# Loads of the mixed up-projection weights issued from ACT's queue instead of SP's

## The chip, the cores and the metric

The kernel runs on one core of a Trainium2 chip. The metric is the device time of one execution in microseconds; the kernel before takes 936.96 us in the median of three runs (936.65 to 940.6). The engines are named as in the profile: PE (matrix products), PEld (PE's weight loads), DVE, ACT, POOL, and SP, which computes nothing and issues DMAs. An engine's name with a q (SPq, ACTq) is its sequencer, which waits for semaphores and issues DMAs.

## The reference

Attention with random features, and a feed-forward pair of products behind it:

```python
q_s, k_s = (q * scale, k * scale)
def phi(x):
    proj = np.einsum('bhsd,md->bhsm', x, omega)
    sq = np.sum(x * x, axis=-1, keepdims=True) / 2.0
    h = proj - sq
    h = h - np.max(h, axis=-1, keepdims=True)
    return np.exp(h) / np.sqrt(m)
q_p, k_p = (phi(q_s), phi(k_s))
kv = np.einsum('bhsm,bhsd->bhmd', k_p, v)
z = np.sum(k_p, axis=2)
num = np.einsum('bhsm,bhmd->bhsd', q_p, kv)
den = np.einsum('bhsm,bhm->bhs', q_p, z)[..., None] + 1e-06
x = (num / den).transpose(0, 2, 1, 3).reshape(B * S, H * D)
h = x @ w_in
return np.maximum(0.01 * h, h) @ w_out
```

There are 8 batches of 576 tokens, 8 heads of 64, 128 features; x is 4608 by 512, w_in 512 by 2048, w_out 2048 by 512. Everything is float32 outside; inside, each float32 number is held as two float16 parts, and a product is three float16 products.

## The kernel before, in words

The 4608 tokens go in nine blocks of 512 (`NB`). For each block the kernel makes attention features of keys and queries (`Unit`, `key_batch`, `query_block`), turns the result so that the model dimension lies on the partitions, multiplies by w_in (up), applies the leaky ReLU and multiplies by w_out (down). Blocks 0 to 2 use plain products (line 1268). From block 3 (`FIRST_S`) on the up-projection uses seven products of half-size blocks in place of eight (`seven_products`, line 1178 the matrix products); from block 8 the down-projection does so too (line 1102, otherwise line 1292).

The seven products need sums and differences of blocks of w_in. `mixed_weights` makes them once and writes them, split into float16 parts, to a scratch in DRAM, `w1s` (line 979 and a line before it). `seven_products` reads them back in every block from 3 on: for each of four column groups `phi` it loads four tiles of kind "wt", two of 128 by 1024 and two of 128 by 768 words of four bytes (line 1161, in `loaded`). One group is held over to the next block, so there are 76 such loads. They go into tiles whose last readers are products of an earlier group, so a load waits for PE; the first nine also wait for the scratch.

In a group `phi` of `seven_products` three PSUM banks take turns. Product 1 goes into bank "c", and ACT or DVE copies it out (`keep`, line 375 in `high`); product 2 goes into "a"; product 6 goes into "c" again, and so on. The copy out of "c" and the next use of "c" are thus one product apart, which is 12 matrix products. What is copied out is added to other products by DVE (line 1193), passes the leaky ReLU on ACT (line 1201, or 375 and 1201), and is split into two float16 parts, the second one on POOL or DVE (line 381).

DMAs that turn a tile (DMA_TRANSPOSE) are on the way of attention: line 604 turns the scaled keys or queries into `att_t`, of which there is one tile, that PE reads in line 618; line 864 turns query features (`att_qp`); line 830 turns the attention result (`fix_xt`). All of them, the loads of keys, queries and values (lines 573, 716), the writes of the result (lines 1301, 1128) and the 76 loads of line 1161 are issued by SP.

The order of everything is computed at build time by `Plan.order`: each operation has a cost on each engine, and the plan takes the operation that can start first; `op("SP", 0.45, ...)` books 0.45 us on SP. The engines' instruction streams are then written out in that order, each engine running its own stream strictly in order and waiting on semaphores for the others. Completion of DMAs is told by eight semaphores used in turn, so that a DMA also waits for the one eight places before it in the order written out.

Of the kernel before, what the change touches and what calls it, by code (L numbers as in the profile page):

```python
# [95 lines left out]
class Plan:  # L96
# [17 lines left out]
    def buf(self, kind):  # L114
        b = Buf(kind)
        self.kinds.setdefault(kind, []).append(b)
        return b
# [166 lines left out]
def act(n, pointers=0):  # L284
    return 0.19 + n / 1190 + 0.09 * pointers


def dve(n):
    return 0.15 + n / 930
# [15 lines left out]
def performer_ffn(ctx: ExitStack, tc, qT, kT, qn, kn, vn, omT, eye, w_in, w_out, out):  # L305
    nc = tc.nc
# [54 lines left out]
    def op(engine, cost, run, port=False, **of):  # L361
        return ways([(engine, cost, run, port or engine == "POOL")], **of)

    def high(n, dst, src, scale=None, psum=False, **of):

        pointer = scale is not None and not isinstance(scale, float)
        value = (lambda: scale()) if pointer else (lambda: scale)

        def dve_run():
            if scale is None:  # L370
                nc.vector.tensor_copy(dst(), src())
            else:
                nc.vector.tensor_scalar(dst(), src(), value(), None, op0=ALU.mult)
        return ways([
            ("ACT", act(n, int(pointer)), lambda: nc.scalar.activation(dst(), src(), AF.Copy,  # L375
             scale=1.0 if scale is None else value()), False),
            ("DVE", dve(n) if psum else dve2(n), dve_run, not psum)], **of)

    def low_(n, dst, a, b, engines=("DVE",), **of):

        return ways([(e, c, lambda g=g: g.tensor_tensor(dst(), a(), b(), op=ALU.subtract), True)  # L381
                     for e, c, g in (("POOL", pool_(n), nc.gpsimd), ("DVE", stt(n), nc.vector)) if e in engines], **of)

    def at(b):
        return tiles[b.kind][b.place]
# [68 lines left out]
    class Weight:  # L454
# [92 lines left out]
        def keys(self, i):  # L547
            return [(self.parts[i], 0), (self.parts[i], 1)]
# [389 lines left out]
    def unit(tile_, u):  # L938

        return tile_.bitcast(F16).rearrange("p (u i f) -> p u i f", u=4, i=2)[:, u]  # L940
# [206 lines left out]
    def seven_products(j, gs, part, top, work, finish=None):  # L1147

        turn = turn_of(j)
        banks_, rows_, sets = {}, {}, {}
        if turn[0] in held_w1s:
            sets[turn[0]] = held_w1s.pop(turn[0])

        def loaded(phi):
            if phi not in sets:
                sets[phi] = [buf("wt") for _ in range(4)]
                for q in range(4):
                    n = 1024 if q % 2 == 0 else 768  # L1160
                    op("SP", 0.45, lambda q=q, n=n: nc.sync.dma_start(out=at(sets[phi][q])[:, :n],
                       in_=w1s[4 * phi + q, :, :n]), r=[("w1s", phi, q // 2, x) for x in UNIT if UNIT[x][0] == q % 2],
                       w=[sets[phi][q]], prio=0.0, moved=P * n * 4)
            return sets[phi]

        def product(phi, n, bank, first=False, last=False):
            q, u = UNIT[n]
            wb = [loaded(phi)[2 * c + q] for c in range(2)]
            if (phi, bank) not in banks_:
                banks_[phi, bank] = buf("ffn")  # L1170
            b = banks_[phi, bank]

            def run():
                for a in range(2):
                    o, i = at(b)[:, 256 * a:256 * a + 256], 0
                    for c in range(2):
                        for wp, xp in ((0, 0), (0, 1), (1, 0)):
                            nc.tensor.matmul(o, unit(at(wb[c]), u)[:, wp, P * a:P * a + P], mixes[j, c][n][1](xp),  # L1178
                                             start=(first and a == 0 and i == 0), stop=(a == 1 and i == 5),
                                             skip_group_check=True)  # L1180
                            i += 1
            plan.like("ffn", 1.5)
            op("PE", 12 * 0.1095, run, r=[*wb, mixes[j, 0][n][0], mixes[j, 1][n][0]], w=[b], prio=work)
            plan.like()
            return b

        def keep(b):
            g = buf("row")
            high(512, lambda: at(g), lambda: at(b), psum=True, r=[b], w=[g], prio=top - 1.0)
            return g  # L1190

        def added(g, b):
            op("DVE", dve(512), lambda: nc.vector.tensor_tensor(at(g), at(g), at(b), op=ALU.add), r=[b], w=[g], prio=top - 1.0)  # L1193

        def done(g, src, phi, side, h):

            f = 8 * side + 2 * phi
            out = lambda i: at(gs[f // 4]).bitcast(F16).rearrange("p (f i t) -> p f i t", f=4, i=2)[
                :, f % 4:f % 4 + 2, i, 256 * h:256 * h + 256]
            wide = lambda: at(g).rearrange("p (f t) -> p f t", f=2)  # L1200
            op("ACT", act(512), lambda: nc.scalar.activation(at(g), at(src), AF.Prelu, scale=H_DOWN_D if finish else H_DOWN_S,  # L1201
               alpha=0.01),
               r=[src], w=[g], prio=top - (0.0 if src is g else 0.5))
            if finish:
                finish(g, phi, side, h)
                return
            keys = lambda i: [(gs[f // 4], x, i, h) for x in (f, f + 1)]
            high(512, lambda: out(0), wide, r=[g], w=keys(0), prio=top)
            low_(512, lambda: out(1), wide, lambda: out(0), r=[g, *keys(0)], engines=("POOL", "DVE"), w=keys(1), prio=top)

        ones_ = {turn[0]: keep(product(turn[0], 1, "c", True))}
        for phi, next_ in zip(turn, (*turn[1:], None)):
            s1 = ones_[phi]
            b = product(phi, 2, "a", True, True)
            added(s1, b)
            done(s1, s1, phi, 0, 0)
            u2 = keep(product(phi, 6, "c"))
            d = product(phi, 7, "d", True)
            w = keep(product(phi, 5, "c"))
            added(w, d)  # L1220
            done(w, w, phi, 1, 1)
            if next_ is not None:
                ones_[next_] = keep(product(next_, 1, "c", True))
            c12, b = buf("row"), product(phi, 3, "c", last=True)
            done(c12, b, phi, 0, 1)
            b = product(phi, 4, "d", last=True)
            added(u2, b)
            done(u2, u2, phi, 1, 0)
        held_w1s[turn[3]] = sets[turn[3]]
# [9 lines left out]
    def turn_of(j):  # L1239

        return (0, 1, 2, 3) if (j - FIRST_S) % 2 == 0 else (3, 2, 1, 0)
# [162 lines left out]
```

## Time and profile before

| | |
|---|---|
| median of 3 runs | 936.96 us (936.65 to 940.6) |
| the profiled execution's own time | 939.2 us |
| its span, first to last instruction | 937.4 us |
| PE busy | 917.6 us, 98% |
| DVE, ACT, POOL busy | 709.3, 581.2, 416.6 us (76%, 62%, 44%) |
| granted TensorE clock | 0.998 |
| DMA moved | 145.92 MB, mean 156 GB/s |

The busy times say which engine has least room. The chain of waits follows the last instruction back through what released it. The list of waits says for how long an engine stood idle and what ended it. The timeline shows instructions in order of time, merged where equal ones follow each other; the bracket behind a row is the idle time before it and what ended it. For SP a row lasts from its first issue to the end of its last one, and a DMA's landing is not in it.

### The profile page before, as it was taken

Reading aid. Unit: us, or ns where it says so; the run is one execution under the profiler, and the core shown is the slowest. Engines: PE = TensorE matmul, PEld = TensorE weight load, DVE = VectorE, ACT = ScalarE, POOL = GpSimd, SP = SyncE. Lnnn points to the kernel's source line nnn. Section 1 sums busy time; section 2 is a strip of 40 time slices with the busy share of each in tenths; the row PEclk is TensorE's granted clock in tenths of the full one; section 3 lists DMA queues with packets and bytes.
Section 4 is the critical chain, followed back from the end, with each engine's and each line's share of the span. In section 5 each row is a group of like instructions: output and inputs, shape, how many; then the busy total and the mean of one; then the engine's idle time right before and its main releaser. Section 6 shows DMA issues by size and latency. Waiting matters only on the chain.

```text
span 937.4 us, 21163 instructions
## 1 busy us (share of the span) xinstructions
PE 917.6 (98%) x8608; PEld 612.7 (65%) x8608; DVE 709.3 (76%) x1275; ACT 581.2 (62%) x866; POOL 416.6 (44%) x380
## 2 busy tenths in 40 slices
PE   8899999999999999999999999999998999999998
PEld 6789455555555445578557855785577647845887
DVE  7789987878996877989888897876878421285773
ACT  4778777657764876568656864687567514622650
POOL 2332633557657664226332554247024722574541
PEclk9999999999999999999999999999999999999999
DMA  9754547583576789789777977496849832721301
GB/s 362 254 182 142 173 113 175 101 200 88 116 170 144 163 170 225 180 182 230 158 140 161 246 176 141 130 238 152 163 115 226 174 79 94 195 57 31 133 1 45
DMA packets 257729, 145.92 MB, mean 156 GB/s; under 512 B 191328, under 2 KB 237152, under 8 KB 256608
## 3 DMA queue, kind: packets, MB, share of 16 engines
q1 hardware_dynamic: 257632, 144.58, 63.8%
q8 instruction: 67, 1.10, 0.5%
q14 instruction: 30, 0.25, 0.1%
HBM read 81.36 MB, written 16.78 MB: 105 GB/s over the span
## 4 chain that ended last, share of the span: by engine, by line
PE 86%; DVE 6%; DMA 5%; issue 1%; ACT 1%; SPq 0%; POOL 0%; DVEq 0%; ACTq 0%
PE fixps_ffn L1292 31%; PE fixps_ffn L1178 19%; PE fixps_ffn L1268 11%; PE attps_pj L618 5%; PE lateps_ffn L1292 3%; PE lateps_ffn L1178 3%; PE lateps_ffn L1102 2%; DMA fix_big<-w_in 2%; PE fixps_ffn L1102 2%; PE attps_mi L785 2%; DVE fix_wt L495 2%; PE attps_pj L682 1%; PE attps_mi L895 1%; DMA att_t<-att_z 1%; DMA fix_xt<-fix_xn 1%
## 5 line engine op out<-in xcount | busy, mean ns | idle before, releaser
L1292 PE MATMUL fixps_ffn<-fix_wt,fix_big 128*128 128x512 f16 x1392 | 313.1, 379 | 0.0
L381 POOL TENSOR_TENSOR fix_big<-fix_row,fix_big 128x512 f16<-128x512 f32 x132 | 164.8, 1257 | 215.1 <-ACT fix_big L375 202.1
L1292 PEld LDWEIGHTS <-fix_big 128*128 128x128 f16 x1536 | 145.6, 98 | 166.2
L1178 PEld LDWEIGHTS <-fix_wt 128*128 128x128 f16 x2016 | 194.7, 98 | 26.4 <-issue 1.3
L1178 PE MATMUL fixps_ffn<-fix_xt,fix_wt 128*128 128x256 f16 x1800 | 204.5, 273 | 0.9 <-DVE fix_row L1193 0.9
L1268 PE MATMUL fixps_ffn<-fix_xt,fix_wt 128*128 128x512 f16 x576 | 129.5, 379 | 0.1
L637 ACT ACTIVATE att_p<-att_p,shift 128x1024 f32<-128x1024 f32 (+1 forms) x68 | 69.6, 1029 | 44.7 <-DVE att_p L634 44.7
L1268 PEld LDWEIGHTS <-fix_wt 128*128 128x128 f16 x576 | 54.6, 98 | 62.4
L381 DVE TENSOR_TENSOR att_ph<-att_p,att_ph 128x1024 f16<-128x1024 f32 x56 | 76.7, 1370 | 16.0 <-ACT att_ph L375 14.4
L375 ACT ACTIVATE fix_big<-fix_row 128x512 f16<-128x512 f32 x138 | 83.6, 621 | 7.5 <-DVE att_sc L584 3.6
L381 POOL TENSOR_TENSOR fix_xn<-fix_x,fix_xn 128x512 f16<-128x512 f32 (+1 forms) x36 | 43.6, 1210 | 98.8 <-ACT fix_xn L375 96.2
L625 DVE TENSOR_REDUCE att_st<-attps_pj 128x8 f32<-128x1024 f32 x68 | 73.0, 1074 | 15.1 <-PE attps_pj L618 14.9
L1193 DVE TENSOR_TENSOR fix_row<-fix_row,fixps_ffn 128x512 f32<-128x512 f32 x64 | 43.8, 684 | 50.0 <-PE fixps_ffn L1178 26.4
L634 DVE SCALAR_TENSOR_TENSOR att_p<-attps_pj,att_sc,att_st 128x1024 f32<-128x1024 f32 x68 | 76.7, 1132 | 0.4
L375 ACT ACTIVATE att_ph<-att_p 128x1024 f16<-128x1024 f32 x56 | 58.6, 1047 | 2.1 <-PE attps_mi L799 1.2
L576 ACT ACTIVATE att_z<-att_nat 128x512 f32<-128x512 f32 (+1 forms) x56 | 36.2, 646 | 33.9 <-DMA att_t<-att_z 26.8
L1201 ACT ACTIVATE fix_row<-fix_row 128x512 f32<-128x512 f32 x70 | 43.6, 624 | 17.5 <-DVE fix_row L1193 17.2
L618 PE MATMUL attps_pj<-om,att_t 64*128 64x128 f16 x1416 | 50.1, 217 | 4.4 <-DMA att_t<-att_z 4.4
L578 DVE TENSOR_REDUCE att_sq<-att_z 128x8 f32<-128x512 f32 (+1 forms) x56 | 39.4, 707 | 19.0 <-ACT att_z L576 18.7
L618 PEld LDWEIGHTS <-att_t 64*128 64x128 f16 x1416 | 39.7, 94 | 20.6 <-issue 13.3
L375 ACT ACTIVATE fix_row<-fixps_ffn 128x512 f32<-128x512 f32 x62 | 36.7, 592 | 24.7 <-PE fixps_ffn L1178 21.2
L375 ACT ACTIVATE fix_row<-fixps_ffn,fix_s 128x512 f32<-128x512 f32 x28 | 19.1, 684 | 50.0 <-PE fixps_ffn L1292 50.0
(187 smaller groups left out, 1645.8 us busy)
## 6 DMA issues: line engine op xcount, KB each, us to landing
fix_wt<-w1s SPq DMA_DIRECT2D x38, 512.0 KB, 4.7
fix_wt<-w1s SPq DMA_DIRECT2D x38, 384.0 KB, 3.6
att_v<-vn SPq DMA_DIRECT2D x16, 650.0 KB, 5.4
out<-fix_row SPq DMA_DIRECT2D x35, 256.0 KB, 2.3
fix_big<-w_in SPq DMA_DIRECT2D x8, 1024.0 KB, 11.3
fix_big<-w_out SPq DMA_DIRECT2D x8, 1024.0 KB, 5.2
att_nat<-qn SPq DMA_DIRECT2D x32, 256.0 KB, 3.2
w1s<-fix_y SPq DMA_DIRECT2D x32, 128.0 KB, 2.4
```

What stands on the lines that cost most here:

```text
L375: ("ACT", act(n, int(pointer)), lambda: nc.scalar.activation(dst(), src(), AF.Copy, scale=1.0 if scale is None else value()), False),
L381: return ways([(e, c, lambda g=g: g.tensor_tensor(dst(), a(), b(), op=ALU.subtract), True) for e, c, g in (("POOL", pool_(n), nc.gpsimd), ...
L578: op("DVE", dve(n), lambda: nc.vector.tensor_reduce(at(self.sq).rearrange("p (h c) -> p c h", h=2)[:, :nt], square().rearrange("p (c h d) ...
L618: nc.tensor.matmul(at(pj)[:, 512 * h + c * M:512 * h + (c + 1) * M], at(self.t)[r, 2 * (c0 + c) + x, :], om[r, w, :], start=(x + w == 0), ...
L625: op("DVE", dve(n * M), lambda: nc.vector.tensor_reduce(row(0), pv(), axis=AX.X, op=ALU.max), r=[pj], w=[st], prio=prio)
L634: op("DVE", dve(n * M), lambda: nc.vector.scalar_tensor_tensor(p(), pv(), down(), row(2).rearrange("p (g o) -> p g o", o=1).broadcast_to([ ...
L637: op("ACT", act(n * M, 1), lambda: nc.scalar.activation(flat(p()), flat(p()), AF.Exp, bias=shift), w=[p32], r=["ones"], prio=prio)
L1178: nc.tensor.matmul(o, unit(at(wb[c]), u)[:, wp, P * a:P * a + P], mixes[j, c][n][1](xp), start=(first and a == 0 and i == 0), stop=(a == 1 ...
L1193: op("DVE", dve(512), lambda: nc.vector.tensor_tensor(at(g), at(g), at(b), op=ALU.add), r=[b], w=[g], prio=top - 1.0)
L1201: op("ACT", act(512), lambda: nc.scalar.activation(at(g), at(src), AF.Prelu, scale=H_DOWN_D if finish else H_DOWN_S, alpha=0.01), r=[src], ...
L1268: nc.tensor.matmul(at(ph), wk[wp][:, c:c + P], xt[:, xp, :], start=(i == 0), stop=(i == 3 * KT - 1))
L1292: nc.tensor.matmul(at(po), part(f, gp)[:, t * P:(t + 1) * P], wf[wp], start=(n == 0 and f % 4 == 0 and gp == wp), stop=(n == 3 and f % 4 = ...
```

## The change

In `loaded`, the call that issues the load names the scalar engine (ACT) in place of the sync engine (SP). The planner's entry is left: the operation is still planned as 0.45 us on SP, so the order written out of all operations is the same, and only the stream into which the 76 DMA instructions go differs.

```diff
                 for q in range(4):
                     n = 1024 if q % 2 == 0 else 768
-                    op("SP", 0.45, lambda q=q, n=n: nc.sync.dma_start(out=at(sets[phi][q])[:, :n],
+                    op("SP", 0.45, lambda q=q, n=n: nc.scalar.dma_start(out=at(sets[phi][q])[:, :n],
                        in_=w1s[4 * phi + q, :, :n]), r=[("w1s", phi, q // 2, x) for x in UNIT if UNIT[x][0] == q % 2],
```

The streams of PE, DVE and POOL hold the same instructions in the same order as before. SP's stream, in the stretch between 731 and 815 us of the trace, before; `fix_xt` are turned attention results, `fix_wt` the tiles of the mixed weights:

```order
L1301 DMA out<-fix_row_2_94 128x512
L1301 DMA out<-fix_row_4_96 128x512
L1161 DMA fix_wt_1_65<-w1s_123 128x768
L1161 DMA fix_wt_7_71<-w1s_123 128x1024
L1161 DMA fix_wt_3_67<-w1s_123 128x768
L1161 DMA fix_wt_16_80<-w1s_123 128x1024
L1161 DMA fix_wt_5_69<-w1s_123 128x768
L1161 DMA fix_wt_11_75<-w1s_123 128x1024
L1161 DMA fix_wt_9_73<-w1s_123 128x768
L1161 DMA fix_wt_12_76<-w1s_123 128x1024
L1161 DMA fix_wt_1_65<-w1s_123 128x768
L1161 DMA fix_wt_3_67<-w1s_123 128x1024
```

and SP's stream from the same place after the change:

```order
L1301 DMA out<-fix_row_2_94 128x512
L1301 DMA out<-fix_row_4_96 128x512
L830 DMA_TRANSPOSE fix_xt_0_98<-fix_xn_0_86 128x4x128
L830 DMA_TRANSPOSE fix_xt_1_99<-fix_xn_1_87 128x8x128
L830 DMA_TRANSPOSE fix_xt_3_101<-fix_xn_0_86 128x8x128
```

The loads are gone from SP's stream, and the turning of `fix_xt` follows the writes of the result at once.

ACT's stream, at the first four of these loads (about 786 us), before; `fixps_ffn` are PSUM banks:

```order
L375 ACTIVATE fix_row_0_92<-fixps_ffn_1_112 128x512
L375 ACTIVATE fix_row_3_95<-fixps_ffn_0_111 128x512
L1201 ACTIVATE fix_row_0_92<-fix_row_0_92 128x512
L1201 ACTIVATE fix_row_2_94<-fixps_ffn_1_112 128x512
L375 ACTIVATE fix_big_1_89<-fix_row_0_92 128x2x256
L375 ACTIVATE fix_big_0_88<-fix_row_2_94 128x2x256
L1201 ACTIVATE fix_row_5_97<-fix_row_5_97 128x512
```

and after:

```order
L375 ACTIVATE fix_row_0_92<-fixps_ffn_1_112 128x512
L1161 DMA fix_wt_1_65<-w1s_123 128x768
L1161 DMA fix_wt_7_71<-w1s_123 128x1024
L375 ACTIVATE fix_row_3_95<-fixps_ffn_0_111 128x512
L1201 ACTIVATE fix_row_0_92<-fix_row_0_92 128x512
L1201 ACTIVATE fix_row_2_94<-fixps_ffn_1_112 128x512
L375 ACTIVATE fix_big_1_89<-fix_row_0_92 128x2x256
L375 ACTIVATE fix_big_0_88<-fix_row_2_94 128x2x256
L1161 DMA fix_wt_3_67<-w1s_123 128x768
L1161 DMA fix_wt_16_80<-w1s_123 128x1024
L1201 ACTIVATE fix_row_5_97<-fix_row_5_97 128x512
```

The first pair now stands directly ahead of a copy out of a PSUM bank, the second ahead of a leaky ReLU. At 703 us of the trace a pair that stood on SP ahead of two turnings of `att_qp` and `att_t` goes into ACT's stream in the same way:

```order
L375 ACTIVATE att_ph_167<-att_p_1_165 128x1024
L1161 DMA fix_wt_73<-w1s 128x768
L1161 DMA fix_wt_80<-w1s 128x1024
L1201 ACTIVATE fix_row_95<-fix_row_95 128x512
L1201 ACTIVATE fix_row_93<-fix_row_93 128x512
```

Here the pair follows the copy of the query features (`att_ph`), and a leaky ReLU comes behind it.

## Rows read from the trace of the kernel before

**Rows 1.** The page's busy times (part 1: busy us, share of the span, instructions) and its chain by engine (part 4).

```profile
PE 917.6 (98%) x8608; PEld 612.7 (65%) x8608; DVE 709.3 (76%) x1275; ACT 581.2 (62%) x866; POOL 416.6 (44%) x380
...
PE 86%; DVE 6%; DMA 5%; issue 1%; ACT 1%; SPq 0%; POOL 0%; DVEq 0%; ACTq 0%
```

**Rows 2.** The list of waits, of PE alone: who waited for whom, us in total, times, longest.

```profile
PE attps_pj L618 <- DMA att_t<-att_z: 4.4, 3, 2.8
...
PE fixps_ffn L1178 <- DVE fix_row L1193: 0.9, 1, 0.9
```

**Rows 3.** The timeline of PE at its three longest stops behind 328 us: start, us, what; in brackets the idle time before.

```profile
500.43 0.78 PE L618 MATMUL attps_pj<-om,att_t 64*128 64x128 f16 x21 [0.84 <-DMA att_t<-att_z]
...
549.33 0.92 PE L1178 MATMUL fixps_ffn<-fix_xt,fix_wt 128*128 128x256 f16 x7 [0.85 <-DVE fix_row L1193]
...
712.79 0.84 PE L618 MATMUL attps_pj<-om,att_t 64*128 64x128 f16 x24 [2.79 <-DMA att_t<-att_z]
```

**Rows 4.** The chain of waits in order of time at two of these stops: start, us, what.

```profile
536.33 4.41 DMA fix_xt<-fix_xn
...
542.10 2.37 DVE att_v L381
...
703.45 0.78 PE attps_pj L618 x24
704.23 2.43 PE fixps_ffn L1178 x22
706.65 6.10 DMA att_t<-att_z
```

**Rows 5.** The waits of SP's own sequencer.

```profile
SPq L1161 <- PE fixps_ffn L1178: 63.3, 23, 7.2
...
SPq L604 <- PE attps_pj L618: 31.5, 18, 3.5
```

**Rows 6.** The timeline of SP in four stretches.

```profile
492.85 1.23 SPq L864 DMA_TRANSPOSE att_qp<-att_ph  x1
494.17 1.51 SPq L830 DMA_TRANSPOSE fix_xt<-fix_xn  x1
495.79 1.26 SPq L604 DMA_TRANSPOSE att_t<-att_z  x1
...
533.90 1.03 SPq L1161 DMA_DIRECT2D fix_wt<-w1s  x2
535.03 2.75 SPq L830 DMA_TRANSPOSE fix_xt<-fix_xn  x2
...
703.60 1.00 SPq L1161 DMA_DIRECT2D fix_wt<-w1s  x2
704.70 1.84 SPq L864 DMA_TRANSPOSE att_qp<-att_ph  x1
706.65 4.01 SPq L604 DMA_TRANSPOSE att_t<-att_z  x1
...
786.26 19.15 SPq L1161 DMA_DIRECT2D fix_wt<-w1s  x10
805.96 2.71 SPq L830 DMA_TRANSPOSE fix_xt<-fix_xn  x2
```

**Rows 7.** The instructions of line 1161, and those of line 604: duration of an issue in ns (least, median, most), first and last start; and the time from issue to landing.

```profile
L1161 SPq DMA_DIRECT2D fix_wt<-w1s x76: 319/388/1765, 328.1 to 879.1; - x76
...
DMA to landing us min/median/max: 2.9/4.2/7.9
...
L604 SPq DMA_TRANSPOSE att_t<-att_z x56: 1231/1258/4523, 102.7 to 745.1; - x56
...
DMA to landing us min/median/max: 3.0/3.5/8.7
```

**Rows 8.** The timeline of ACT where pairs of loads enter its stream: at 625, 702 and 786 us.

```profile
624.64 0.71 ACT L375 ACTIVATE att_z<-att_nat,att_sc 128x512 f16<-128x512 f32 x1
625.79 0.60 ACT L375 ACTIVATE fix_row<-fixps_ffn 128x512 f32<-128x512 f32 x1 [0.43 <-PE fixps_ffn L1178]
...
701.89 1.05 ACT L375 ACTIVATE att_ph<-att_p 128x1024 f16<-128x1024 f32 x1
702.89 0.63 ACT L1201 ACTIVATE fix_row<-fix_row 128x512 f32<-128x512 f32 x1
...
786.60 0.60 ACT L375 ACTIVATE fix_row<-fixps_ffn 128x512 f32<-128x512 f32 x1 [1.50 <-PE fixps_ffn L1178]
787.91 0.60 ACT L375 ACTIVATE fix_row<-fixps_ffn 128x512 f32<-128x512 f32 x1 [0.71 <-PE fixps_ffn L1178]
```

**Rows 9.** Busy time (and count) by stretch, of the stretches in which the loads are issued: span, its length, PE, PEld, DVE, ACT, POOL, granted clock, DMA share, GB/s.

```profile
405.00:447.00 42.00, 42.00 (x528) 36.87 (x527) 36.44 (x70) 34.95 (x59) 21.29 (x20) 1.00 0.84 208
500.00:546.00 46.00, 45.57 (x542) 38.27 (x543) 38.03 (x66) 38.63 (x61) 22.80 (x20) 1.00 0.89 213
595.00:636.00 41.00, 41.00 (x478) 35.77 (x477) 32.93 (x60) 35.13 (x57) 18.76 (x18) 1.00 0.86 208
690.00:731.00 41.00, 38.21 (x446) 33.82 (x444) 29.66 (x53) 30.31 (x51) 19.70 (x18) 1.00 0.80 200
782.00:815.00 33.00, 32.93 (x309) 29.21 (x308) 7.57 (x13) 21.93 (x39) 15.66 (x14) 1.00 0.62 183
```

**Rows 10.** The chain of waits at 863 us: one product of line 1178, 12 matrix products.

```profile
863.40 1.31 PE fixps_ffn L1178 x12
```

## The prediction

> **What bounds the kernel.** I read the page's busy times first, then the chain of waits, then the list of waits, then the timelines of PE, SP and ACT. The busy times say PE: 917.6 of 937.4 us [rows 1], and the chain agrees, 86% of it being PE's own work. So nothing that only shortens a DMA or a queue can give more than PE's stops. Behind 328 us, where the first of the loads is issued [rows 7], the list of waits and the timeline give three stops worth naming: 0.84 us at 500, 0.85 us at 549 and 2.79 us at 713 [rows 2, 3], together 4.5 us. That is 0.48% of the time, and it is the ceiling of the gain.
>
> Two of the stops lead back to SP. At 713 PE waits for the turned keys or queries `att_t`. The chain goes from the landing at 712.75 back over 6.10 us of DMA to the issue at 706.65 [rows 4]. SP's timeline shows what stood there: a pair of the loads at 703.60, a turning of `att_qp` at 704.70, and then the issue of `att_t` at 706.65, which itself took 4.01 us [rows 6] against a median of 1.258 [rows 7]. The landing took 6.10 us against a median of 3.5. At 549 the chain goes through DVE back to a turning of `fix_xt` issued at 536.33 [rows 4], the second of two that stand right behind a pair of loads at 533.90 [rows 6]. The stop at 500 follows a turning issued at 495.79 that stands behind other turnings and no load of line 1161 [rows 6]. I give it no gain.
>
> **What goes from SP.** 76 issues of 0.388 us in the median (29 us of SP), and with them 63.3 us in which SP stood at one of them waiting for PE [rows 5], while later turnings stood behind it. The plainest place is 786 to 805 us, where ten loads hold SP for 19.15 us and two turnings of `fix_xt` come out at 805.96 [rows 6].
>
> At 713: without the pair, `att_qp` can be issued about 1.0 us earlier, and `att_t` behind it. `att_t` has one tile, which PE reads from 703.45 on [rows 4]; so the turning can't start before about 703.5, and with an issue of `att_qp` of 1.2 us ahead of it starts at about 704.2. That is 2.4 us before the 706.65 of now. If the landing still takes 6.10 us, the stop shrinks from 2.79 to about 0.35; if the landing falls towards 3.5 us, since the 0.9 MB of loads (128 by 1792 words of four bytes) are no longer ahead of it in the same queue, the stop goes. Gain 2.4 to 2.79; I take 2.6. Its other end is nothing, should the transfers share the same DMA time anyway.
>
> At 549: the turning comes 1.03 us earlier, the time of the pair, and the 0.85 us stop goes if everything on DVE between them (the chain has 2.37 us of `att_v` there) moves too. Gain 0 to 0.85; I take 0.5.
>
> **What comes onto ACT.** 76 issues. The trace shows none on ACT. The nearest row is SP's own: 0.319 at least, 0.388 in the median, 1.765 at most [rows 7]. A pair back to back took 0.80 to 1.03 us on SP [rows 6]. Lower bound nothing (issued while an ACTIVATE is still running), upper bound 1.765 each; I take the median, and 0.82 us a pair, since it is the same instruction.
>
> What hides it. In the stretches where the loads are issued ACT is busy 34.95 of 42, 38.63 of 46, 35.13 of 41, 30.31 of 41 and 21.93 of 33 us [rows 9], so 6 to 11 us idle, while six pairs want 4.9 us. And the pairs stand where ACT waits for PE: at 786 the pair comes behind a copy that ends at 787.20 and ahead of one that starts at 787.91 after 0.71 us of idling; at 625 the room is 0.43 us [rows 8]. If the issue may begin while the copy runs, another 0.5 us is room. A pair of 0.82 us then fits in 0.9 to 1.2; if it may not, it is late by 0.1 to 0.4 us. A late copy out of bank "c" costs PE only what goes over the room left: one product of 1.31 us [rows 10] lies between, of which the copy takes 0.60. So some 0.7 us less two hand-overs, about 0.4 us, is left. Queued behind the DMA on ACT are the copies, leaky ReLUs and high parts that DVE, POOL and PE take next. I put the whole toll at 0 to 1.5 us and take 0.6.
>
> The added wait. On ACT a load stands still until PE has read the old weights. At 786 its place is reached at about 786.7, when SP had already been able to issue it (786.26) [rows 6, 8]. At 702 ACT comes to the pair by 702.9, and SP issued it at 703.60; whether PE had let go of the tiles by then no row says, so up to 0.7 us of waiting is possible there. The plan orders ACT by the same times by which it ordered the loads, so I take no waiting. The weights land 4.2 us after issue in the median and PE has not one stop on `fix_wt<-w1s` in its list of waits; an issue some tenths later should stay hidden.
>
> **The sum.** 2.6 + 0.5 - 0.6 = 2.5 us less. Against the profiled execution's own 939.2 us (span 937.4 and 1.8 around it) that is 936.7. The median of the runs is 936.96, 2.2 us under that execution; if its stops are the same, the sum gives 934.5, and if the profiled execution was long because of its stop at 713, the gain is mostly not there to have and the time stays near 936.7. I take the middle, 935.6 us.
>
> **Rivals.**
>
> A, the forecast: turnings come earlier, one or two stops go, ACT pays little. 933 to 936.5 us. Chance 0.42.
>
> B, nothing to be measured: what is taken off SP is not what the stops wait for, because the DMA engines are shared and are 0.80 to 0.89 busy in those stretches [rows 9]; gain and toll cancel, 936.5 to 938. For it: PE's ceiling is small. Against it: the issue of 4.01 us and the place right behind a pair. The Trainium skill, in "DMA: Bandwidth & Descriptors" (Issuing engines are not separate DMA queues), says that all issuers' transfers run on the same 16 DMA engines and that issuing from several saves only the sequencer's time. By that rule the landing of 6.10 us would stay and only the 2.4 us of issue would be gained. No run here yet shows two issuers. Chance 0.28.
>
> C, the other side: issuing costs ACT far more than it cost SP, and copies out of PSUM come late. Place: the pairs directly ahead of a copy out of a bank, some 14 of the 38 by the order. Price: if each load has to wait for one turning of SP, 1.23 us [rows 7], a pair is 2.46 us; less 1.2 us of room and 0.4 us at PE it costs 0.86 us each, 12 us in all, or 949 us; at 1.765 us each it is 1.9 us each and 27 us, 964. It decides from about 0.8 us a load on. For it: the turnings ahead of the stop at 713 keep SP issuing for 1.84 and 4.01 us [rows 6], so the two issuers would often meet, and ACT is idle for only 14 to 17% of three stretches [rows 9]. Against it: SP's median of 0.388. The Trainium skill, in "Perfetto Trace Analysis" (DMA Instruction — HWDGE (DVE, Sync)), says that the block that makes the descriptors is shared, is locked by one issuer at a time, and that the wait for the lock is within the profiled interval. No trace here shows that yet; if it holds, it is what would make C true. Chance 0.22.
>
> D, contention: the loads, now beside the turnings and not ahead of them, slow each other. PE's waits for `att_t` double, 4.4 us more: 941. For it the DMA share; against it that no byte is added. Chance 0.06. That the change doesn't do what it says is excluded by the order: 76 rows left SP, 76 came to ACT. The remaining 0.02 I leave to what I don't see.
>
> **How the numbers follow.** What a measurement of this kernel can tell from no change is about 0.5%: below 932.3 us or above 941.6. Faster than that needs nearly all of the 4.5 us of stops without any toll; I give it 0.10, all from A. Slower comes from C (all but 0.02), half of D and the unseen: 0.24. The rest is 0.66. The range of 8 in 10 goes from 932, where all stops are gone, to 944, which takes in A, B, D and the mild part of C.
>
> **What would show it.** Right: PE's stop on `att_t` at 713 gone or under 0.5 us; issue of `att_t` there at about 704; line 1161 under ACTq with a median near 0.4 us; ACT's idling before copies unchanged within some tenths. Wrong: ACTq issues of 0.8 us and more, and a new line in PE's list of waits that names ACT `fix_row` L375; or PE waiting for `fix_wt<-w1s`; or the stop at 713 still there with `att_t` issued early, which would be B.

## The result and the profile after

The changed kernel takes 950.1 us in the median (948.4 to 959.8, four runs) against 936.9: a ratio of 1.0149, with a 95% interval of 1.0121 to 1.0177. It is 1.5% slower; the prediction of 935.6 us and its range up to 944 us were wrong. The profiled execution took 949.1 us (span 947.3), 9.9 us of span more than the one of before. The ratios and intervals in this document are those on record; a quotient of the medians beside them can differ by 0.002.

First the page of the changed kernel: busy times, the new queue of DMA packets (packets, MB, share of 16 engines' span) and the chain by engine, beside [rows 1].

```profile
PE 919.5 (97%) x8608; PEld 613.7 (65%) x8608; DVE 709.9 (75%) x1275; ACT 580.3 (61%) x866; POOL 418.3 (44%) x380
...
q10 hardware_dynamic: 10944, 34.87, 11.8%
...
PE 81%; DMA 8%; DVE 6%; issue 2%; ACT 2%; SPq 1%; ACTq 0%; DVEq 0%
```

The loads are a second queue, q10, with 34.9 MB. DMA in the chain went from 5% to 8%, PE from 86% to 81%, ACT from 1% to 2%.

Then PE's list of waits behind 328 us, beside [rows 2], and PE's timeline at its longest stops, beside [rows 3].

```profile
PE attps_mi L897 <- DMA att_qp<-att_ph: 5.1, 2, 3.7
PE attps_pj L618 <- DMA att_t<-att_z: 3.8, 4, 1.4
PE attps_pj L618 <- DVE att_p L634: 2.0, 1, 2.0
PE fixps_ffn L1178 <- ACT fix_row L375: 2.0, 2, 1.4
```

```profile
367.64 0.85 PE L618 MATMUL attps_pj<-om,att_t 64*128 64x128 f16 x24 [2.02 <-DVE att_p L634]
...
372.63 0.20 PE L897 MATMUL attps_mi<-fix_kv,att_qp 128*128 128x65 f16 x1 [1.39 <-DMA att_qp<-att_ph]
...
448.15 0.84 PE L618 MATMUL attps_pj<-om,att_t 64*128 64x128 f16 x24 [1.32 <-DMA att_t<-att_z]
...
455.73 0.84 PE L618 MATMUL attps_pj<-om,att_t 64*128 64x128 f16 x24 [1.42 <-DMA att_t<-att_z]
...
716.63 0.20 PE L897 MATMUL attps_mi<-fix_kv,att_qp 128*128 128x65 f16 x1 [3.67 <-DMA att_qp<-att_ph]
...
822.65 1.03 PE L1178 MATMUL fixps_ffn<-fix_xt,fix_wt 128*128 128x256 f16 x8 [1.36 <-ACT fix_row L375]
```

Summed over the trace, PE's stops behind 328 us grew from 4.56 to 12.81 us, by 8.25. The rest is clock. The windows around the longest stop show it (span, its length, PE, PEld, DVE, ACT, POOL, granted clock, DMA share, GB/s).

```profile
712.00:716.00 4.00, 0.96 (x11) 0.76 (x8) 3.93 (x4) 0.83 (x2) 2.69 (x2) 1.00 1.35 180
716.00:720.00 4.00, 3.37 (x28) 2.66 (x29) 1.23 (x5) 0.63 (x2) 0.00 (x0) 0.71 0.88 165
720.00:724.00 4.00, 4.00 (x50) 3.14 (x49) 2.62 (x9) 3.50 (x5) 0.00 (x0) 0.86 0.71 234
```

Behind the stop of 3.67 us the granted clock is 0.71 and 0.86 in two windows of 4 us. At the lower of the two levels, half speed, that is (0.29 + 0.14) x 4 / 0.5 = 3.4 us, in which 1.7 us of work are lost; PE's busy time is 1.9 us larger. The stops ahead of 328 us are 0.3 us shorter, and 8.25 + 1.9 - 0.3 make the 9.9 us. (The medians are 13.2 us apart: the profiled execution of before lies 2.3 us above its median, the one of after 1 us below its own.)

Where do the stops come from? The chain of waits of the changed kernel in order of time, in three places (start, us, what), beside [rows 4].

```profile
353.02 12.00 DMA att_t<-att_z
...
365.05 0.64 ACT att_z L576
...
438.22 1.61 ACTq L1161
...
441.67 13.41 DMA fix_xt<-fix_xn
...
708.13 8.46 DMA att_qp<-att_ph
```

Three turnings land 12.00, 13.41 and 8.46 us after their issue. Each stands beside loads on ACT's queue: five of them at 350.1 to 353.5, two at 437.9 and 438.2 and two more at 444.3 and 444.7, a pair at 708.1. Of the 129 turnings behind 328 us the median landing is 3.6 us (3.5 before), so most are untouched; but six take over 8 us, where before it was one, with 8.65 (the `att_t` that now takes 12.00).

The last place is not the stop of before grown longer. PE waited there for `att_t`; now it waits for the `att_qp` that was issued at 702.19 before, ahead of the pair on SP, and landed after 4.7 us. ACT issues the pair at the same moment as this turning (708.12 and 708.13), and it lands after 8.46 us. SP's timeline, beside [rows 6]:

```profile
705.65 6.24 SPq L864 DMA_TRANSPOSE att_qp<-att_ph  x3
712.00 4.03 SPq L604 DMA_TRANSPOSE att_t<-att_z  x1
```

`att_t` still takes 4.03 us to issue, and lands after 6.7 us (6.10 before), with no load ahead of it on SP's queue.

ACT itself, line 1161 under its own sequencer and the timeline at 708 us, beside [rows 7, 8].

```profile
L1161 ACTq DMA_DIRECT2D fix_wt<-w1s x76: 326/327/1612, 327.6 to 889.0; - x76
```

```profile
707.84 1.05 ACT L375 ACTIVATE att_ph<-att_p 128x1024 f16<-128x1024 f32 x1
708.12 0.81 ACTq L1161 DMA_DIRECT2D fix_wt<-w1s  x2
```

An issue costs 0.327 us in the median, and this pair of 0.81 us lies almost wholly under a running ACTIVATE of 1.05 us. Of the 76 issues 59 begin while an ACTIVATE runs.

So one theory is that the bytes of the loads, on a queue of their own beside SP's turnings, hold these up (overtaking or contention). The rival is that 76 issues in ACT's in-order stream make its copies late (a held ACT): two stops of after do name ACT's `fix_row`. A third is that more DMAs on shared completion counters couple the two engines.

### The profile page after: what moved, and what is told of

It reads as the page before. It is cut to its first block, busy times and chain, and to the rows that moved or that the text cites. A ratio compares the mean times of both kernels' runs of the same rounds, so it can differ in the third digit from the quotient of the medians.

```text
span 947.3 us, 21134 instructions
## 1 busy us (share of the span) xinstructions
PE 919.5 (97%) x8608; PEld 613.7 (65%) x8608; DVE 709.9 (75%) x1275; ACT 580.3 (61%) x866; POOL 418.3 (44%) x380
## 3 DMA queue, kind: packets, MB, share of 16 engines
q10 hardware_dynamic: 10944, 34.87, 11.8%
## 4 chain that ended last, share of the span: by engine, by line
PE 81%; DMA 8%; DVE 6%; issue 2%; ACT 2%; SPq 1%; ACTq 0%; DVEq 0%
PE fixps_ffn L1292 26%; PE fixps_ffn L1178 19%; PE fixps_ffn L1268 12%; PE attps_pj L618 4%; PE lateps_ffn L1292 3%; PE lateps_ffn L1178 2%; DMA att_t<-att_z 2%; PE lateps_ffn L1102 2%; DMA fix_big<-w_in 2%; DMA fix_xt<-fix_xn 2%; PE fixps_ffn L1102 2%; PE attps_mi L785 2%; PE attps_pj L682 1%; DVE fix_wt L495 1%; DMA att_qp<-att_ph 1%
## 5 line engine op out<-in xcount | busy, mean ns | idle before, releaser
L381 POOL TENSOR_TENSOR fix_big<-fix_row,fix_big 128x512 f16<-128x512 f32 x132 | 169.5, 1292 | 214.6 <-ACT fix_big L375 201.1
L381 POOL TENSOR_TENSOR fix_xn<-fix_x,fix_xn 128x512 f16<-128x512 f32 (+1 forms) x36 | 41.6, 1157 | 99.9 <-ACT fix_xn L375 98.6
```

## The experiments

**Issues on ACT without the bytes.** All loads stay on SP; at each place ACT issues a small DMA.

```
-   lambda q=q, n=n: nc.sync.dma_start(out=at(sets[phi][q])[:, :n], in_=w1s[...])
+   lambda q=q, n=n: (nc.sync.dma_start(out=at(sets[phi][q])[:, :n], in_=w1s[...]), tiny())
+   tiny = lambda: [nc.scalar.dma_start(out=bits[:, 4 * c:4 * c + 4], in_=eye[:, :4])
+                   for c in [next(spot) % 16]]
```

> All 76 loads stay on SP, as in the kernel before; at each place where a load is issued, ACT issues a DMA of its own of 128 rows of 16 bytes. The theory of overtaking (the bytes on a second queue hold up the turnings on SP's) expects the time of before within 0.3%, 935 to 940 us, and PE's stops after 328 us at 4 to 6 us. The theory of a held ACT (76 issues in ACT's stream make its copies late) expects most of the loss to be there: 945 us or more, with stops of PE on ACT fix_row. The theory of shared completion counters (more DMAs on the same counters couple SP and ACT) expects something between.

Measured: 939.0 us against 938.2, a ratio of 1.0003 (0.9987 to 1.0020). The row of the small DMAs:

```profile
L1145 ACTq DMA_DIRECT2D bits<-eye x76: 334/353/1173, 325.1 to 875.9; - x76
```

76 issues on ACT, each as long as the loads' own, cost nothing that can be told; PE's stops behind 328 us are 4.16 us. The time of the issues and the counters fall as causes of the 1.5%. A held ACT is not yet excluded by this: the small DMAs do not wait for PE, as the loads do.

**The changed kernel with few bytes, and the same from SP.** From the ninth load on only 16 of 128 rows are moved.

```
-   lambda q=q, n=n: nc.scalar.dma_start(out=at(sets[phi][q])[:, :n], in_=w1s[4 * phi + q, :, :n])
+   lambda q=q, n=n, p=P if j == 3 and phi < 2 else 16: nc.scalar.dma_start(
+       out=at(sets[phi][q])[:p, :n], in_=w1s[4 * phi + q, :p, :n])
```

> Loads on ACT as in the changed kernel, with the same issues and the same waits, but from the ninth load on each moves only 16 of its 128 rows (the weights in the other rows stay those of an earlier load, so the output is not the reference's). Overtaking expects PE's stops behind 437 us to go, some 9 us with the lost clock at 717; only the two at 365 and 371 (3.4 us) stay: 939 to 942 us. A held ACT expects 946 us or more, since ACT issues and waits as before.

> The same small loads (16 of 128 rows from the ninth on, output not the reference's) issued from SP, as a base for the run with small loads on ACT. Every theory expects 933 to 938 us: the bytes ahead of the turnings at 703 us are gone, so at most PE's stop of 2.79 us at 713 goes.

Measured: 935.9 us from ACT, a ratio of 0.9962 (0.9946 to 0.9978), and 934.3 us from SP, 0.9959 (0.9944 to 0.9974). ACT issues and waits as in the changed kernel, and the whole loss is gone, so a held ACT falls too. Without the bytes the two queues are 1.5 us apart in the median, where with them it was 13. The expectation of 939 to 942 was too high: of the stops at 365 and 371 only one of 0.81 us is left, at 367. Of the five loads there all but the last kept their bytes, and the turning beside them lands after 9.35 us, not 12.00 (8.65 before).

**Parts of the change.** First all loads but those of the first block with mixed weights on ACT, then only those.

```
-   nc.sync.dma_start(
+   (nc.scalar if j >= 4 else nc.sync).dma_start(      # and: if j == 3
```

> The first 16 loads and the burst at 350 us (all of the first block with mixed weights, j = 3) on SP, the other 60 on ACT. Overtaking expects the stops at 365 to 475 us (7.5 us) to go and the ones at 713 (3.67 us and about 1.7 us of clock) and 821 (1.36 us) to stay: 941 to 944 us. A held ACT expects a loss in proportion to the issues, 60 of 76 of 13 us: about 947 us.

> Only the loads of the first block with mixed weights (j = 3, 16 of 76) on ACT, the rest on SP. The theory of overtaking expects the stops at 365 to 475 us (7.5 us in the changed kernel) and not the ones at 518, 713 and 821: 943 to 946 us. A cost by the number of issues expects 16 of 76 of the loss, 939 to 940.

Measured: 949.7 us with the late ones, a ratio of 1.0114 (1.0083 to 1.0145), and 943.0 us against 937.6 with the first block alone, 1.0056 (1.0036 to 1.0077). The second is at the edge of the 943 to 946 of the contention and above the 939 to 940 by the number of issues, but not by the stops expected: the one at 365 is there, with 3.17 us, those of the changed kernel from 440 to 476 are not. The first is above the expected 941 to 944. PE's timeline and the chain of the late loads on ACT tell why:

```profile
525.06 1.46 PE L618 MATMUL attps_pj<-om,att_t 64*128 64x128 f16 x24 [6.68 <-DMA att_t<-att_z]
```

```profile
512.36 12.66 DMA att_t<-att_z
```

A stop of 6.68 us stands at 518, where the changed kernel has none: the turning `att_t`, issued at 512.36, meets a pair issued 0.81 us later, at 513.17, and lands after 12.66 us. From 520 to 528 us the granted clock is 0.57, which is 6.9 us at half speed. In the changed kernel the same turning is issued at 520.41 and its pair 1.13 us later, and it lands after 3.9 us. What collides is decided by some tenths of a microsecond, so the stops cannot be added up place by place, as I had done.

**The loads from POOL.** Neither SP nor ACT issues them.

```
-   nc.sync.dma_start(
+   nc.gpsimd.dma_start(
```

> All 76 loads issued from POOL, so neither SP nor ACT issues them. If it is the second queue beside SP's turnings that costs, the loss comes again although ACT has nothing more to do: 945 to 955 us, stops of PE on att_t and att_qp. If it were ACT's issuing, it would be gone: 935 to 939 us. POOL is busy 44%, and its issuing may cost it more than SP's 0.39 us; then PE's or DVE's waits name POOL.

Measured: 949.9 us against 937.6, a ratio of 1.0153 (1.0119 to 1.0186): the loss of the changed kernel, with ACT's stream as it was before. Line 1161 under POOL, and PE's waits behind 328 us in this kernel (the profiled execution is its fastest, 944.6 us):

```profile
L1161 POOL DMA_DIRECT2D fix_wt<-w1s x76: 533/551/735, 326.8 to 884.8; - x76
```

```profile
PE attps_mi L897 <- DMA att_qp<-att_ph: 4.7, 2, 3.1
PE attps_pj L618 <- DMA att_t<-att_z: 2.3, 3, 1.3
PE fixps_ffn L1178 <- ACT fix_row L375: 1.4, 1, 1.4
```

The turnings head the list again. The wait on ACT's `fix_row`, 1.4 us at 817, is here as well, so it is not ACT's issuing that makes it. The chain shows what does: in the first row before, in the others the changed kernel.

```profile
805.96 5.17 DMA fix_xt<-fix_xn
...
814.48 6.47 DMA fix_xt<-fix_xn
...
820.97 0.03 ACT fix_xn L375
...
822.12 0.49 ACT fix_row L375
```

ACT, in order, stands at a copy until this turning has landed, and only then comes to the one that PE waits for. In the four runs with a stop of 1.3 to 1.5 us here (the change, late loads on ACT, loads on POOL, first block on ACT) the turning lands after 6.3 to 6.6 us; with 5.7 us (small DMAs on ACT) the stop is 0.6, with 5.2 to 5.4 us (before, pairs moved) at most 0.3. With the first block alone SP itself issues the loads here, the last of them 0.6 us ahead of the turning instead of 0.9. So this stop does not need the second queue; the distance is the likely cause, but no run varied it alone. POOL's own cost (0.551 us an issue) is not separated from this.

**One queue and two, by themselves.** A program of DMAs alone, each case four times, VectorE reading the whole target between cases.

```
def turning_then_pair_one_queue():
    nc.sync.dma_start(out=t, in_=flat(z[:, :10]), transpose=True)
    nc.sync.dma_start(out=x[:, 0:1024], in_=big)
    nc.sync.dma_start(out=x[:, 1024:1792], in_=mid)
def turning_and_pair_two_queues():
    nc.sync.dma_start(out=t, in_=flat(z[:, :10]), transpose=True)
    nc.scalar.dma_start(out=x[:, 0:1024], in_=big)
    nc.scalar.dma_start(out=x[:, 1024:1792], in_=mid)
```

> A program of its own that computes nothing of the reference. Four times over, with DVE reading the whole target between any two cases: one turning (128 x 1280 two-byte words) on SP alone; a pair of loads (128 x 1024 and 128 x 768 words of four bytes) alone; turning then pair on SP; pair then turning on SP; turning on SP and pair on ACT; a plain copy in pieces of 256 bytes alone and beside a pair on ACT; one load on each of SP and ACT; the pair cut into pieces of 512 bytes, alone and on ACT beside a turning. Plain sharing of the same DMA engines expects that turning and pair on two queues are both done after the sum of their times alone, as on one queue, some 7 to 8 us. The theory that the two disturb each other beyond sharing expects 10 to 13 us, as in the run with the late loads on ACT (att_t 12.66 us, its pair 11.2 us), and two loads on two queues at no more than on one. Whether the plain copy in pieces behaves like the turning tells whether the turning or only the small packets matter.

The turning's rows by line: alone (L322), ahead of a pair on one queue (L329), behind a pair on one queue (L336), beside a pair on two (L339).

```profile
L322 SPq DMA_TRANSPOSE x<-z x4: 1327/1342/1370, 18.0 to 398.5; - x4
DMA to landing us min/median/max: 3.3/3.4/3.5
...
L329 SPq DMA_TRANSPOSE x<-z x4: 1327/1347/1357, 40.8 to 421.3; - x4
DMA to landing us min/median/max: 3.3/3.3/3.4
...
L336 SPq DMA_TRANSPOSE x<-z x4: 1981/2056/2127, 55.4 to 436.1; - x4
DMA to landing us min/median/max: 5.3/5.3/5.4
...
L339 SPq DMA_TRANSPOSE x<-z x4: 1338/1342/1350, 68.1 to 449.0; - x4
DMA to landing us min/median/max: 6.1/6.6/7.7
```

On one queue a turning ahead of the pair lands as if alone (3.3 us); on two, with the pair issued at the same moment, after 6.6 us. On one queue all is done after 6.3 us (40.79 to 47.1), on two after 6.1 to 7.7. That is the plain sharing of the DMA engines, and it does not yet give 12.66 us. The other cases share as well: a plain copy in pieces lands after 3.2 to 3.3 us alone and 6.0 to 6.1 beside a pair, one load on each queue after 4.3 to 4.8, and the turning beside a pair cut into pieces of 512 bytes after 6.3 to 6.5.

**When the pair arrives.** An ACTIVATE of so many elements holds the pair back on ACT; in some cases SP issues a load of 128 x 640 words (the form of `att_nat`) ahead of the turning, as at 512 us in the kernel.

```
def hold(n):
    nc.scalar.activation(a[:, 0:1], seen, AF.Copy)
    if n:
        nc.scalar.activation(a[:, 0:n], x[:, 0:n], AF.Copy)
def after_rows_pair_held_700():
    hold(700)
    nc.sync.dma_start(out=nat, in_=rows)
    nc.sync.dma_start(out=t, in_=flat(z[:, :10]), transpose=True)
    nc.scalar.dma_start(out=x[:, 0:1024], in_=big)
    nc.scalar.dma_start(out=x[:, 1024:1792], in_=mid)
```

> A program of its own that computes nothing of the reference, for the landing of 12.66 us that is not yet explained (in the program with one and two queues the turning beside a pair landed after 6.1 to 7.7 us). A turning of 128 x 1280 two-byte words on SP, and on ACT a pair of loads that an ACTIVATE of 0, 256, 700, 1300 or 1792 elements holds back, so that it arrives before, during or behind the turning's own transfer; the same with a load of 128 x 640 words (att_nat's form) ahead of the turning, and with VectorE copying beside it; and all of it on one queue. If a pair that arrives while the turning moves is what disturbs it, some offset gives 10 to 13 us; if the load ahead of the turning does, the cases with it give that at any offset; if it is the memory traffic of the engines, only the case with VectorE's copies does. If none of them does, 6 to 8 us everywhere, the 12.66 us stays open.

Without the load ahead, the turning lands after 6.9, 5.9, 3.6, 3.4 and 3.4 us (medians, held by 0 to 1792). With it and a hold of 700, in the first row, it takes 10.4; on one queue, in the second, 4.1.

```profile
L370 SPq DMA_TRANSPOSE x<-z x4: 1266/1388/1491, 120.5 to 597.0; - x4
DMA to landing us min/median/max: 8.4/10.4/12.1
...
L396 SPq DMA_TRANSPOSE x<-z x4: 1266/1389/1513, 170.3 to 647.9; - x4
DMA to landing us min/median/max: 4.0/4.1/4.2
```

The windows over the slowest of the four such cases on two queues and over one on one queue (span, length, DVE, ACT, POOL, clock, DMA share, GB/s):

```profile
120.10:133.40 13.30, 0.00 (x0) 0.97 (x2) 0.00 (x0) 1.00 0.90 118
...
169.80:177.00 7.20, 0.01 (x1) 0.00 (x0) 0.00 (x0) 1.00 0.73 218
```

The same bytes take 13.3 us at 118 GB/s on two queues (9.5 to 13.2 in the four) and 7.2 us at 218 on one (6.8 to 7.5). This is worse than sharing: the engines are 0.90 busy and move half as much. The load ahead is part of it: with the pair issued 0.69 us behind the turning (a hold of 256) and no load ahead the turning lands after 5.9 us, with it and 0.63 us (a hold of 700) after 10.4. VectorE's copies beside it changed nothing (4.4 us, against 4.5 without), but only at a hold of 1300, where nothing collapses.

**Turning or small pieces.** The same with more offsets, and with a plain copy in pieces of 256 bytes in the turning's place.

```
-   nc.sync.dma_start(out=t, in_=flat(z[:, :10]), transpose=True)
+   nc.sync.dma_start(out=pieces, in_=z[:, :10])
```

> A program of its own that computes nothing of the reference. A load of 128 x 640 words and then a turning on SP, the pair on ACT held back by 256, 500, 700, 900 and 1100 elements; in the same way a plain copy in pieces of 256 bytes in the turning's place, held by 500, 700 and 900; the load alone beside the pair; and load, pieces and pair on one queue. The run before gave 10.4 us (8.4 to 12.1) for the turning at 700, 7.1 at 0 and 4.5 at 1300. If arriving while the turning starts to move is what disturbs, the slow landings stand in a band of offsets around 700 and fade to both sides. If the turning itself is needed, the pieces stay at 6 to 7 us at every offset; if two queues with pieces of different size suffice, they reach 9 us or more as well.

The turning at a hold of 500 (L338) and the pieces at the same hold (L366):

```profile
L338 SPq DMA_TRANSPOSE x<-z x6: 1252/1606/1827, 42.3 to 878.8; - x6
DMA to landing us min/median/max: 11.8/12.3/13.8
...
L366 SPq DMA_DIRECT2D x<-z x6: 626/626/710, 112.8 to 949.3; - x6
DMA to landing us min/median/max: 6.9/7.2/7.6
```

The turning's medians are 11.8, 12.3, 11.0, 7.7 and 6.1 us at holds of 256, 500, 700, 900 and 1100: a band, as expected, with 7.1 us at a hold of 0 in the program before. In its slow part the pair is issued 0.2 to 0.6 us behind the turning. The pieces stay at 6.9 to 7.4 (4.1 to 4.9 on one queue, ahead of the pair). So at these offsets two queues with pieces of different size only share; of what was tried, only the turning collapses, and only behind a load on its own queue.

**All on SP, a pair behind the turnings.** If bytes ahead of a turning count, the pair at 703 us in the kernel before is to go behind the two turnings that follow it; then also the pair at 534.

```
+   of_order = sorted(mixed_loads, key=order.index)
+   for pair in (of_order[29:31], of_order[47:49]):        # first run: [47:49] alone
+       behind = [o for o in order[order.index(pair[1]) + 1:]
+                 if "SP" in o.ways and o.ways["SP"][0] == 1.25][:2]
+       for o in pair:
+           order.remove(o)
+       place = order.index(behind[1]) + 1
+       order[place:place] = pair
```

> All loads on SP as before, but the pair at 703 us is issued behind the two turnings that follow it (att_qp, att_t), so that these have neither its issue nor its bytes ahead of them. Overtaking (bytes ahead of or beside a turning decide) expects PE's stop of 2.79 us at 713 to go to under 0.5 us and the time to fall by 2 to 2.8 us, a ratio of 0.997 to 0.998, provided PE does not then wait for fix_wt. If the stop comes from elsewhere (ACT's or DVE's work ahead of the turnings), the time stays.

> As the run with the pair at 703 us behind its turnings, and the pair at 534 us behind the two turnings of fix_xt that follow it as well. In the prediction the second pair had a term of 0.5 us (stop at 549, 0.85 us). If the pair held the turning, the stop at 549 goes or falls; the chain of the run with one pair moved shows the turning waiting for POOL until 535.0 us, and by that the stop stays at 0.85 us. In either case the ratio is 0.997 to 0.999.

Measured: 935.8 us against 937.6, a ratio of 0.9981 (0.9971 to 0.9992), with one pair, and 934.5 us against 938.0, 0.9962 (0.9948 to 0.9975), with two. SP's timeline and PE's longest wait behind 328 us with two pairs moved:

```profile
534.20 2.58 SPq L830 DMA_TRANSPOSE fix_xt<-fix_xn  x2
536.83 1.05 SPq L1161 DMA_DIRECT2D fix_wt<-w1s  x2
...
705.09 1.24 SPq L604 DMA_TRANSPOSE att_t<-att_z  x1
706.38 1.05 SPq L1161 DMA_DIRECT2D fix_wt<-w1s  x2
```

```profile
PE attps_pj L618 <- DMA att_t<-att_z: 0.9, 1, 0.9
```

The issue of `att_t` at 705 takes 1.24 us where it took 4.01 [rows 6], and the stops at 549 and 713 are gone; PE's stops behind 328 us are 1.36 us. I had expected the one at 549 to stay, from a chain that led to POOL; it went. This kernel is faster than both, and as fast as the one whose small loads on SP move almost nothing (934.3 us), so what is left to gain from the loads' place is too small to tell.

## Why the prediction was wrong

**What bounds the kernel** was right: PE, and only its stops could change the time. The ceiling of 4.5 us for the gain held; no variant gained more (0.41% with small loads).

**The toll on ACT**, 0 to 1.5 us with 0.6 taken, was right in size: 76 issues gave 1.0003 (0.9987 to 1.0020). Most begin under running ACTIVATEs (59 of 76 in the changed kernel), which the prediction left open. One long issue, 1.61 us at 438, did make a copy late, and PE stopped for 0.62 us at 440.

**Rival C** named the side that came, and its 949 to 964 us hold the result, but by chance: its price of 1.23 to 1.765 us a load was 0.327, and its mechanism was excluded by the small loads on ACT and by the loads from POOL. The Trainium skill's sentence on the shared block that is locked by one issuer ("Perfetto Trace Analysis", DMA Instruction — HWDGE (DVE, Sync)) would fit the few long issues, but not the median; and in the program of DMAs alone the turning's issue on SP takes 1.342 us in the median both alone and with two issues on ACT inside it (L322, L339).

**The step that failed** is the landing at 713. The prediction put it between "still takes 6.10 us" and "falls towards 3.5 us", since the loads "are no longer ahead of it in the same queue", and its lower end was a gain of nothing, "should the transfers share the same DMA time anyway". A loss was not in these bounds. In the changed kernel this `att_t` lands after 6.7 us, with no load ahead of it in its queue. And the pair, on a queue of its own, no longer comes behind the `att_qp` that stood ahead of it on SP: it is issued with it, and that turning takes 8.46 us instead of 4.7. PE's stop here went from 2.79 to 3.67 us and was followed by half the clock; new stops from late turnings stand at 365, 371, 447, 454 and 821. By themselves a turning and a pair issued together give 6.6 us instead of 3.3, and behind another load 8.4 to 13.8 us when the pair is issued 0.2 to 0.6 us after the turning.

The earlier issue was mis-sized too. The tile of `att_t` is free when PE has read it, at 704.23 [rows 4] and not at 703.5, and an `att_qp` issued at 703.6 for 1.2 us leads to 704.8, not 704.2. From the issue of the `att_qp` two places ahead to that of `att_t` it was 4.46 us before, 3.87 in the changed kernel (0.6 us gained, not 2.4), and 2.85 and 3.77 with one and two pairs moved. With the pairs moved it is the landing that fell, to 3.6 and 3.1 us.

About the kernel before, the terms of 2.6 and 0.5 us were right in size: a pair ahead on the same queue makes both stops, and moving the pairs behind took both away. What was wrong is that another queue is the same as no pair ahead.

**The middle of the two sums.** The profiled execution of before was long mainly for another reason than its stop at 713: its granted clock was 0.57 from 35 to 39 us, ahead of the first of the 76 loads, which is 1.7 of the 2.3 us above its median. And the chance of slower, with all of the unseen, adds up to 0.25, not 0.24.

**Rival D** was the mechanism. Its term was mis-sized: 4.4 us, from doubling PE's waits for `att_t` alone, and a chance of 0.06. Measured, the stops behind 328 us grew by 8.25 us, and the clock took another 1.7 us. PE's own waits for `att_t` hardly grew (3.6 to 3.8 us); 5.1 us came on `att_qp`, and 2.0 and 1.4 us behind a late `att_t` and a late `fix_xt` by way of DVE and ACT. "No byte is added" was no argument against it, since the rate fell; the bytes did not rise.

**Rival B**'s rule from the Trainium skill ("DMA: Bandwidth & Descriptors", Issuing engines are not separate DMA queues), that issuing from several engines saves sequencer time and no more, agrees where the loads are small (0.9962 and 0.9959 from the two) and for plain pieces. For loads beside turnings the measurement differs and decides: the order is lost, and the rate can halve (218 to 118 GB/s).

**The places 786 to 805**, where I saw ten loads hold two turnings, gave nothing: in the changed kernel the same turning is still issued only when PE is done with the tile that it writes (the chain goes from PE over SP to an issue at 814.48, and before PE let the turning go only at 805.9).

**Not settled**: why a turning behind a load and a pair on another queue fall to half the rate in a band of offsets, why the load ahead is needed, and what made the one long issue on ACT at 438. The late turning behind the stop at 816 to 821 is not taken apart either.

## What to carry to other kernels

A queue is an order as well as a cost: before moving a transfer to another engine's queue, look at what used to be held behind it on the old one, and whether that is what the bound engine waits for. Where a transposing DMA is on the critical path, keep bulk loads that may be late on its queue and place them behind it; this gave 0.4% here, where a second queue lost 1.5%. A sum over places misses what a shift by tenths of a microsecond brings together. To tell an issue's cost from its bytes', run it once with few bytes, and once with a second, small transfer in the new place while the bytes stay in the old one.

## What was not expected of the hardware

- A turning of 327 KB and a pair of loads of 0.9 MB, behind a load of 0.3 MB: 7.2 us at 218 GB/s on one queue, 13.3 us at 118 GB/s with the pair on a second one (9.5 to 13.2 in four cases). Without the load ahead the turning landed after 3.4 to 6.9 us; a plain copy in pieces of 256 bytes instead of the turning after 6.9 to 7.4 us on two queues.
- ACT's issue of a DMA began while an ACTIVATE was running (708.12, within one from 707.84 to 708.89); 76 small DMAs on ACT cost nothing that could be measured (1.0003).
- A stop of 3.67 us was followed by some 3.4 us at half of TensorE's clock, and one of 2.88 us in the run with the late loads on ACT came with as much (0.66 from 715 to 720 us); at the stop of 2.79 us in the kernel before the clock stayed at 1.00.
